# Hardware loops on VectorE and ScalarE, and an earlier V load for nine units, in a two-layer decode kernel

## The chip, the cores and the metric

One NeuronCore of one Trainium2 chip runs the whole program. The metric is the device time in microseconds (us) of one execution; the smaller the better. A program on one core has no second core to be compared with, so every run used here is one that was classed as fast (all executions of a kernel lie within 0.12% of each other). "The span" is the time of the one profiled execution; it is 1 to 2 us shorter than the timed runs.

## The reference, cut to what matters

Two layers of decoding for two sequences, one new token each. Attention over a cache of 16,384 positions in 32 heads dominates: every K and every V is read once per layer and used for one query only.

```python
B, Sq, D = 2, 1, 576
H, Sk, Dh = 32, 16384, 128
def _A_ref(x, k_cache, v_cache, wq, wo):
    q = (x @ wq).reshape(B, Sq, H, Dh)...          # transposed to b h q d
    scores = einsum("bhqd,bhkd->bhqk", q, k_cache) * (Dh ** -0.5)
    o = einsum("bhqk,bhkd->bhqd", softmax(scores), v_cache)
    return o... @ wo
x = x + A(layernorm(x));  x = x + B(layernorm(x))  # B: a small MLP with w1..w4
x = x + A(layernorm(x));  x = x + B(layernorm(x))  # the same caches and weights again
```

One (sequence, head) pair is called a unit: 64 units per layer, with 4 MB of K and 4 MB of V each (bfloat16).

## The kernel before

A unit's K is transposed on TensorE in chunks of 1024 positions, copied out by ScalarE (ACT) and multiplied with the query on TensorE; the remaining chunks are multiplied and summed on VectorE (DVE), two instructions per chunk. Then come the maximum, two exponentials on ACT, and the product with V on TensorE one unit later. SBUF holds three places for a K and a V each; K of a unit can be loaded only when the K that lay in its place has been used up.

The program is recorded as a list of operations for each engine and then emitted. TensorE's list is folded into a hardware loop of two units per turn; all other engines get straight-line code. That is the part that the change touches:

```python
ENGS = ("sync", "scalar", "tensor", "vector", "gpsimd")
...
with self.nc.Block() as block:
    for e in self.ENGS:
        def run(eng, items=plan[e], loops=self.loops if e == "tensor" else ()):
            at = 0
            for first, n, period, every, rest in loops:
                ...                                  # straight-line code up to unit `first`
                with eng.Fori(0, n) as turn:         # n turns of two units
                    for o, waits in self._fold(...):
                        self._run(eng, o, [(s, v + turn * d if d else v) for s, v, d in waits])
                    ...                              # every fourth turn: one piece of the wo product
            for o, waits in items[at:]:
                self._run(eng, o, waits)             # straight-line: the rest, or everything
```

The other part is the order of the loads. Layer 1 loads K of unit i, then V of unit i-1. Layer 2 starts with K and V of a unit together for the units 0 to EARLY-1 and then goes over to the order of layer 1; at that point one V is skipped, since it is there already:

```python
EARLY = 5
ROT = 7
...
for i in range(U):
    kv("K", l, i, ...)
    if l == 1 and i < self.EARLY:
        kv("V", l, i)
    elif i >= 1 and (l, i - 1) != (1, self.EARLY - 1):
        kv("V", l, i - 1)
...
def place(self, l, i):          # where K and V of unit i lie
    ...
    return (2, 0, 1)[i % 3] if i < self.ROT else (2, 1)[i % 2]
...
first = (2, self.ROT - 1)[l]    # TensorE's loop starts at unit 2 in layer 1, at unit 6 in layer 2
early = l == 1 and 1 <= i < self.EARLY   # V of unit i-1 is used in the middle of unit i
```

## Time and profile before

| | before |
|---|---|
| time, median of 6 runs | 2578.07 us (2577.16 to 2578.94) |
| span of the profiled run | 2576.8 us |
| read from HBM | 1097.7 MB |
| busy: DVE, PE, ACT | 68%, 64%, 48% of the span |
| rate in most of the 40 slices | 430 to 432 GB/s |

First, lines of the page: the span; what the 16 DMA engines moved in each of 40 equal slices; and the queues of part 3. Queue q1 is the data; q8 and q14, "instruction" by the page's name, carry the instructions that the engines fetch (packets, MB, share of the span of 16 DMA engines).

```profile
span 2576.8 us, 80453 instructions
...
GB/s 413 430 427 432 432 430 432 431 431 432 432 431 431 432 430 432 432 431 431 420 381 408 431 432 431 431 432 431 431 431 432 431 431 431 430 432 431 431 431 340
...
q1 hardware_dynamic: 46712, 1097.76, 99.4%
q8 instruction: 44, 0.72, 0.1%
q14 instruction: 38, 0.31, 0.0%
```

A flat rate: 431 GB/s but at the start, in slices 20 to 22, counted from 1 (the boundary of the layers and a hole 100 us later), and at the end. 1097.7 MB at 431 GB/s is 2547 us. In this trace no slice has more than 432 GB/s, and the packets of q1 take 99.4% of the time of the 16 DMA engines. The instruction queues: 1.03 MB, 0.1% of the DMA engines' time.

The chain of waits through one unit in the steady part (start, duration, what). It begins where a K landed and ends where the load that replaces it was issued, 14.54 us later. A unit takes 19.45 us to load, so compute has slack.

```profile
1440.24 1.89 PE tps L714 x16
...
1454.73 0.02 SPq L163
1454.75 0.03 issue
1454.78 25.70 DMA buf<-in_A_k_cache_dram
```

The same chain at the two ends: the last K of layer 1 lands at 1261.7 us and the last K of layer 2 at 2527.25 us (TensorE starts at once). From there a fixed tail of compute leads to the end at 2576.8.

```profile
1217.92 43.80 DMA buf<-in_A_k_cache_dram
1261.71 0.05 issue
1261.76 1.89 PE tps L714 x16
...
2484.40 42.85 DMA buf<-in_A_k_cache_dram
2527.25 0.05 issue
2527.30 1.89 PE tps L714 x16
```

The windows view of two holes in the loads (stretch, length; busy time and count of PE, PEld, DVE, ACT, POOL; clock, DMA share, GB/s). The first is the MLP between the layers, the second comes 100 us later:

```profile
1290.00:1295.00 5.00, 1.80 (x29) 1.68 (x30) 1.75 (x12) 1.00 (x4) 0.00 (x0) 0.50 0.28 113
1295.00:1300.00 5.00, 4.02 (x144) 3.90 (x141) 0.52 (x3) 0.49 (x2) 0.00 (x0) 0.50 0.48 130
1400.00:1405.00 5.00, 4.61 (x150) 4.35 (x148) 4.93 (x6) 3.36 (x5) 0.00 (x0) 0.84 0.89 377
1405.00:1410.00 5.00, 3.99 (x60) 3.79 (x61) 4.00 (x10) 2.16 (x3) 0.00 (x0) 0.50 0.69 233
```

What no view prints, but the trace holds: each load signals its semaphore sixteen times, and the sixteen times are recorded. The consumer waits for the last: TensorE started on layer 2's last K at 2527.30 us, 0.05 us after its last signal, the median one being 7.9 us older. I call the last signal minus the median one the lag of the latest DMA engine. It is worked out from these records:

```
before: landing of a load (us), and the largest three of the sixteen signals minus their median
  224.9   1.66  0.49  0.13        737.6   4.47  1.74  1.35       1252.1   8.34  3.38  1.76
  489.5   2.48  1.68  0.58        995.0   6.46  2.73  1.77       1310.6   1.61  0.65  0.36
  618.2   3.45  1.70  1.29       1131.9   7.41  3.46  1.80       2527.2   7.90  4.20  1.07
```

One DMA engine falls behind by one us every 128 us or so; at the layer boundary, where the queue runs empty, all catch up (lag 8.4 us at 1289.7, 0.6 at 1303.9), and in layer 2 it begins again. The records do not name the DMA engine of a signal or of a packet: that each of the sixteen signals stands for one of the sixteen engines, and that it is the same engine each time, is inferred from the sizes, which grow in steps.

### The profile page before, as it was taken

The numbers are of one execution on the slowest core, as the hardware profiler recorded it, in microseconds if no ns is written. First come the engines' busy times: TensorE is split into PE (matmuls) and PEld (weight loads), VectorE is DVE, ScalarE is ACT, GpSimd is POOL, SyncE is SP. The second block draws the span as 40 slices with busy tenths as digits, with TensorE's granted clock in tenths as the row PEclk, the third lists the DMA queues.
The fourth block names the chain that finished last, engine by engine and source line by source line (L and its number), as shares of the span: only waits on it lengthen the run. The fifth ranks groups of instructions, "written<-read, shape, count | busy, mean of one in ns | idle before, by whom it ended". The sixth has DMA issues, their size and how long they took to land.

```text
span 2576.8 us, 80453 instructions
## 1 busy us (share of the span) xinstructions
PE 1652.8 (64%) x36879; PEld 1540.8 (60%) x36879; DVE 1749.2 (68%) x2587; ACT 1231.9 (48%) x1941; POOL 0.8 (0%) x10
## 2 busy tenths in 40 slices
PE   5656665666666666666668666566656665666666
PEld 5656655665565656555668666555656565565555
DVE  5666776677666767766659777667766766677664
ACT  4444544454455445544436454445444544454443
POOL 0000000000000000000000000000000000000000
PEclk8666666676667666666656666666666766666666
DMA  9999999999999999999999999999999999999998
GB/s 413 430 427 432 432 430 432 431 431 432 432 431 431 432 430 432 432 431 431 420 381 408 431 432 431 431 432 431 431 431 432 431 431 431 430 432 431 431 431 340
DMA packets 46794, 1098.79 MB, mean 426 GB/s; under 512 B 4916, under 2 KB 6008, under 8 KB 11512
## 3 DMA queue, kind: packets, MB, share of 16 engines
q1 hardware_dynamic: 46712, 1097.76, 99.4%
q8 instruction: 44, 0.72, 0.1%
q14 instruction: 38, 0.31, 0.0%
HBM read 1097.74 MB, written 0.00 MB: 426 GB/s over the span
## 4 chain that ended last, share of the span: by engine, by line
DMA 60%; DVE 29%; PE 9%; issue 1%; ACT 0%; SPq 0%; DVEq 0%
DMA buf<-in_A_k_cache_dram 57%; DVE sd L746 18%; DVE prod L743 10%; PE tps L714 5%; DMA buf<-in_A_v_cache_dram 3%; PE misc L762 1%; PE ops L787 1%; DVE small L764 1%; DMA buf<-in_A_wq_dram 1%; PE sps L584 0%; PE misc L620 0%; ACT ktsb L718 0%; PE sps L731 0%; SPq L405 0%; PE misc L550 0%
## 5 line engine op out<-in xcount | busy, mean ns | idle before, releaser
L718 ACT ACTIVATE ktsb<-tps 128x1024 bf16<-128x1024 bf16 x1156 | 1125.1, 1031 | 872.2 <-PE tps L714 867.1
L714 PE MATMUL tps<-ident,buf 128*128 128x128 bf16 x9248 | 910.1, 262 | 635.0 <-DMA buf<-in_A_k_cache_dram 635.0
L714 PEld LDWEIGHTS tps<-ident,buf 128*128 128x128 bf16 x9248 | 733.7, 120 | 663.3 <-DMA buf<-in_A_k_cache_dram 655.4
L746 DVE TENSOR_REDUCE sd<-prod 128x8 f32<-128x1024 bf16 x892 | 1088.3, 1220 | 30.9
L743 DVE TENSOR_TENSOR prod<-buf,qb 128x1024 bf16<-128x1024 bf16 x892 | 607.9, 682 | 11.3 <-DMA buf<-in_A_k_cache_dram 10.3
L787 PE MATMUL ops<-p,buf 128*128 128x1 bf16 x16384 | 462.4, 164 | 74.9 <-DMA buf<-in_A_v_cache_dram 64.0
L787 PEld LDWEIGHTS ops<-p,buf 128*128 128x128 bf16 x16384 | 444.5, 100 | 84.9 <-DMA buf<-in_A_v_cache_dram 73.5
L764 DVE TENSOR_REDUCE small<-misc 128x1 f32<-128x128 f32 x128 | 37.4, 292 | 666.8 <-PE misc L762 666.8
L731 PE MATMUL sps<-qcur,ktsb 128*128 128x1 bf16 x9248 | 396.9, 166 | 108.8 <-ACT ktsb L718 88.3
L731 PEld LDWEIGHTS sps<-qcur,ktsb 128*128 128x128 bf16 x9248 | 349.0, 101 | 171.2 <-ACT ktsb L718 169.1
L698 ACT ACTIVATE qb<-misc 128x128 bf16<-128x128 f32 x128 | 35.5, 278 | 378.4 <-PE misc L695 378.4
L762 PE MATMUL misc<-identS,small 128*128 128x128 f32 x256 | 95.3, 476 | 13.5 <-DVE small L756 13.5
L762 PEld LDWEIGHTS misc<-identS,small 128*128 128x128 f32 x256 | 69.9, 334 | 15.3 <-DVE small L756 15.1
L773 ACT ACTIVATE p<-sps,small 128x72 bf16<-128x72 f32 (+1 forms) x128 | 41.5, 325 | 8.2 <-DVE small L764 8.2
L773 ACT ACTIVATE p<-sd,small 128x56 bf16<-128x56 f32 (+1 forms) x128 | 44.5, 348 | 0.0
L690 ACT ACTIVATE qcur<-qt 128x1 bf16<-128x1 bf16 x128 | 29.0, 227 | 19.6 <-DVE qt L627 19.6
L695 PE MATMUL misc<-ident,qcur 128*128 128x128 bf16 x128 | 34.2, 267 | 1.1 <-ACT qcur L690 1.1
L856 PE MATMUL misc<-lpiece,small 128*128 128x16 f32 x28 | 8.5, 384 | 36.7 <-DVE lpiece L854 36.7
L856 PEld LDWEIGHTS misc<-lpiece,small 128*128 128x128 f32 x28 | 7.0, 310 | 39.3 <-DVE lpiece L854 39.3
L752 DVE TENSOR_REDUCE small<-sps 128x1 f32<-128x72 f32 (+1 forms) x128 | 28.5, 222 | 0.0
L773 ACT ACTIVATION_READ_ACCUMULATOR p<-sps,small 128x1 f32 x128 | 27.1, 212 | 0.0
L773 ACT ACTIVATION_READ_ACCUMULATOR p<-sd,small 128x1 f32 x128 | 26.5, 207 | 0.0
(86 smaller groups left out, 223.0 us busy)
## 6 DMA issues: line engine op xcount, KB each, us to landing
buf<-in_A_k_cache_dram SPq DMA_DIRECT2D x124, 4096.0 KB, 24.3
buf<-in_A_v_cache_dram SPq DMA_DIRECT2D x124, 4096.0 KB, 34.0
buf<-in_B_w_dram SPq DMA_DIRECT2D x8, 1152.0 KB, 27.1
buf<-in_A_wq_dram SPq DMA_DIRECT2D x8, 1024.0 KB, 10.5
buf<-in_A_wo_dram SPq DMA_DIRECT2D x14, 576.0 KB, 34.6
buf<-in_A_k_cache_dram SPq DMA_DIRECT2D x3, 2048.0 KB, 15.6
buf<-in_B_w_dram SPq DMA_DIRECT2D x2, 2160.0 KB, 34.3
buf<-in_A_v_cache_dram SPq DMA_DIRECT2D x2, 2048.0 KB, 28.0
```

The lines of the kernel that those rows point to most:

```text
L690: self.act(lambda a: a.activation(out=self.qcur[:, q:q + 1], in_=self.qt[:, u:u + 1], func=ACT.Copy), r=["qt"], w=[f"qcur{q}"])
L695: self.pe(lambda pe: pe.matmul(self.misc[:, 0:128], lhsT=bcast(self.qcur[:, q:q + 1], 128), rhs=self.ident[:, :], start=True, stop=True), ...
L698: self.act(lambda a: a.activation(out=self.qb[q][:, :], in_=self.misc[:, 0:128], func=ACT.Copy), r=["P:misc"], w=[f"qb{q}"])
L714: ins = pe.transpose(self.tps[b][:, j * 128:(j + 1) * 128], kt[:, (j0 + j) * 128:(j0 + j + 1) * 128], self.ident[:, :])
L718: self.act(lambda a: a.activation(out=self.ktsb[k][:, :, :].rearrange("p a b -> p (a b)"), in_=self.tps[b][:, :], func=ACT.Copy), r=[f"P:t ...
L731: ins = pe.matmul(self.sps[sp][:, col:col + 1], lhsT=self.ktsb[k][:, j, :], rhs=self.qcur[:, sp:sp + 1], start=True, stop=True)
L743: self.dve(lambda v: v.tensor_tensor(out=self.prod[d][:, :, :], in0=k3, in1=bcast_mid(self.qb[q][:, :], self.CH), op=ALU.mult), r=[*res, f ...
L746: self.dve(lambda v: v.tensor_reduce(out=self.sd[q][:, o:o + self.CH], in_=self.prod[d][:, :, :], axis=AX.X, op=ALU.add), r=[f"prod{d}"], ...
L762: self.pe(lambda pe: pe.matmul(self.misc[:, 128:256], lhsT=bcast(self.m[:, q:q + 1], 128), rhs=self.identS[:, :], start=True, stop=True), ...
L764: self.dve(lambda v: v.tensor_reduce(out=self.bias[:, q:q + 1], in_=self.misc[:, 128:256], axis=AX.X, op=ALU.max, negate=True), r=["P:misc ...
L773: self.act(lambda a, c0=c0, c1=c1, src=src, part=part: a.activation(out=self.p[q][:, c0:c1], in_=src, func=ACT.Exp, bias=self.bias[:, q:q ...
L787: ins = pe.matmul(self.ops[q][:, 0:1], lhsT=vt[:, j * 128:(j + 1) * 128], rhs=self.p[q][:, h * self.TB + j:h * self.TB + j + 1], start=(h ...
```

## The change

The intent: VectorE and ScalarE also get hardware loops (all of a unit's column numbers that vary from turn to turn are held in registers), so that far fewer instructions have to be fetched; and layer 2 loads K and V together for nine units instead of five, to fill the second hole. The diff, cut to its core:

```diff
+    LOOPED = ("scalar", "tensor", "vector")
...
-                def run(eng, items=plan[e], loops=self.loops if e == "tensor" else ()):
+                def run(eng, items=plan[e], loops=self.loops if e in self.LOOPED else ()):
...
-                            for o, waits in self._fold([...]):
-                                self._run(eng, o, [(s, v + turn * d if d else v) for s, v, d in waits])
+                            for o, waits, u in self._fold([...]):
+                                self._run(eng, o, [(s, self._rise(v, turn, d)) for s, v, d in waits],
+                                          u and self._rise(u[0], turn, u[1]))
...
-    EARLY = 5
+    EARLY = 9
...
-        self.act(lambda a: a.activation(out=self.qcur[:, q:q + 1], in_=self.qt[:, u:u + 1], func=ACT.Copy), ...)
+        self.act(lambda a, u: a.activation(out=self.qcur[:, q:q + 1], in_=self.qt[:, bass.ds(u, 1)], ...), ..., u=u)
...                                       # likewise lsum, o, lpiece, opiece: columns from a register
-        first = (2, self.ROT - 1)[l]
+        first = (2, self.EARLY - 1)[l]   # so all loops of layer 2 start at unit 8 instead of 6
...
-            early = l == 1 and 1 <= i < self.EARLY
+            early = l == 1 and 1 <= i < first
```

More of the change, by code (lines that the diff above doesn't have):

```diff
@@ L15, with __init__ @@
 class Op:
-    __slots__ = ("eng", "fn", "deps", "need", "sem", "val", "clock", "at", "tag", "some", "own", "raw")
-    def __init__(self, eng, fn, at, tag, some):
-        self.eng, self.fn, self.at, self.tag, self.some = eng, fn, at, tag, some
+    __slots__ = ("eng", "fn", "deps", "need", "sem", "val", "clock", "at", "tag", "some", "own", "raw", "u")
+    def __init__(self, eng, fn, at, tag, some, u):
+        self.eng, self.fn, self.at, self.tag, self.some, self.u = eng, fn, at, tag, some, u
         self.deps, self.need, self.sem, self.val, self.clock = [], False, None, 0, None
@@ L43, in __init__ @@
         self.some = False
-        self.own = None
         self.loops = []
@@ L55, in _sem, with op @@
         return self.sems[name]
-    def op(self, eng, fn, r=(), w=(), deps=()):
-        o = Op(eng, fn, len(self.ops), self.tag, self.some)
-        if self.own and eng != "tensor":
-            o.own = f"{self.own}_{eng}"
+    def op(self, eng, fn, r=(), w=(), deps=(), u=None):
+        o = Op(eng, fn, len(self.ops), self.tag, self.some, u)
+        if self.some:
+            o.own = f"some_{eng}"
         self.ops.append(o)
@@ L144, in run @@
                             self._run(eng, o, waits)
+                        some = [[x for x in t if x[0].some] for t in turns]
+                        assert [t for t in range(n) if some[t]] in ([], list(range(rest, n, every)))
+                        assert all(o.some for t, c in zip(turns, some) for o, _ in t[len(t) - len(c):])
+                        some = [c for c in some if c]
                         with eng.Fori(0, n) as turn:
-                            for o, waits in self._fold([[x for x in t if not x[0].some] for t in turns]):
-                                self._run(eng, o, [(s, v + turn * d if d else v) for s, v, d in waits])
-                            some = [[x for x in t if x[0].some] for t in turns]
-                            assert [t for t in range(n) if some[t]] == list(range(rest, n, every))
-                            assert all(o.some for t, c in zip(turns, some) for o, _ in t[len(t) - len(c):])
-                            some = [c for c in some if c]
+                            for o, waits, u in self._fold([[x for x in t if not x[0].some] for t in turns]):
+                                self._run(eng, o, [(s, self._rise(v, turn, d)) for s, v, d in waits],
+                                          u and self._rise(u[0], turn, u[1]))
                             if some:
                                 with eng.If((turn + (every - rest)) % every == 0):
-                                    for o, waits in self._fold(some):
-                                        self._run(eng, o, [(s, v + (turn // every) * d if d else v) for s, v, d in waits])
+                                    for o, waits, u in self._fold(some):
+                                        k = turn // every
+                                        self._run(eng, o, [(s, self._rise(v, k, d)) for s, v, d in waits],
+                                                  u and self._rise(u[0], k, u[1]))
                         at = start + sum(map(len, turns))
@@ L159, in emit, with _rise, _run @@
                 getattr(block, e)(run)
-    def _run(self, eng, o, waits):
+    @staticmethod
+    def _rise(v, turn, d):
+        return v + turn * d if d > 0 else v - turn * -d if d else v
+    def _run(self, eng, o, waits, u=None):
         for s, v in waits:
             eng.wait_ge(self.sems[s], v)
-        ins = o.fn(eng)
+        ins = o.fn(eng) if o.u is None else o.fn(eng, o.u if u is None else u)
         if o.sem is not None:
@@ L195, in _fold @@
                 folded.append((s, first, d))
-            body.append((o, folded))
+            us = None
+            if o.u is not None:
+                us = o.u, same[1][0].u - o.u if len(same) > 1 else 0
+                assert all(p.u == us[0] + t * us[1] for t, (p, _) in enumerate(same))
+            body.append((o, folded, us))
         return body
@@ L317, in __init__ @@
         self.wolast = sb("wolast", [128, self.D], BF16)
-        self.lsum = sb("lsum", [128, self.U, 2], FP32)
+        self.lsum = sb("lsum", [128, 2 * self.U], FP32)
         self.o = sb("o", [128, self.U], FP32)
@@ L323, in __init__ @@
         self.lpiece = sb("lpiece", [128, 2 * self.wo_cols], FP32)
+        self.dpiece = sb("dpiece", [128, self.wo_cols], FP32)
         self.opiece = sb("opiece", [128, self.wo_cols], BF16)
@@ L349, in pe, with dve, act @@
     def pe(self, fn, r=(), w=()): return self.s.op("tensor", fn, r, w)
-    def dve(self, fn, r=(), w=()): return self.s.op("vector", fn, r, w)
-    def act(self, fn, r=(), w=()): return self.s.op("scalar", fn, r, w)
+    def dve(self, fn, r=(), w=(), u=None): return self.s.op("vector", fn, r, w, u=u)
+    def act(self, fn, r=(), w=(), u=None): return self.s.op("scalar", fn, r, w, u=u)
     def pool(self, fn, r=(), w=()): return self.s.op("gpsimd", fn, r, w)
@@ L689, in query @@
         u, q = self.order[l][i], i % 2
-        self.act(lambda a: a.activation(out=self.qcur[:, q:q + 1], in_=self.qt[:, u:u + 1], func=ACT.Copy),
-                 r=["qt"], w=[f"qcur{q}"])
+        self.act(lambda a, u: a.activation(out=self.qcur[:, q:q + 1], in_=self.qt[:, bass.ds(u, 1)], func=ACT.Copy),
+                 r=["qt"], w=[f"qcur{q}"], u=u)
     def query_rows(self, l, i):
@@ L772, in exps @@
                                                    (n, self.NB, self.sd[q][:, 0:self.NB - n], f"sd{q}"))):
-            self.act(lambda a, c0=c0, c1=c1, src=src, part=part: a.activation(
+            self.act(lambda a, u, c0=c0, c1=c1, src=src: a.activation(
                 out=self.p[q][:, c0:c1], in_=src, func=ACT.Exp, bias=self.bias[:, q:q + 1], scale=self.scale,
-                accum_out=self.lsum[:, u, part:part + 1]),
-                r=[res, f"bias{q}"], w=[f"p{q}", "lsum"])
+                accum_out=self.lsum[:, bass.ds(u, 1)]),
+                r=[res, f"bias{q}"], w=[f"p{q}", "lsum"], u=2 * u + part)
     def weigh(self, l, i, h):
@@ L793, in weigh @@
         if h == 1 and i < self.U - 1:
-            self.dve(lambda v: v.tensor_copy(out=self.o[:, u:u + 1], in_=self.ops[q][:, 0:1]),
-                     r=[f"P:ops{q}"], w=["o"])
+            self.dve(lambda v, u: v.tensor_copy(out=self.o[:, bass.ds(u, 1)], in_=self.ops[q][:, 0:1]),
+                     r=[f"P:ops{q}"], w=["o"], u=u)
     def normalizers(self, u0, u1):
@@ L800, in normalizers @@
         self.pe(lambda pe: pe.matmul(dps, lhsT=bcast(self.cone[:, :], 128),
-                                     rhs=self.lsum[:, u0:u1, :].rearrange("p u a -> p (u a)"),
+                                     rhs=self.lsum[:, 2 * u0:2 * u1],
                                      start=True, stop=True), r=["lsum", "consts"], w=["P:misc"])
@@ L851, in project_piece @@
         out = self.misc[:, 256:256 + KT * B]
-        den = self.den[:, u0:u1]
-        self.s.some, self.s.own = True, "piece"
-        self.dve(lambda v: v.tensor_copy(out=self.lpiece[:, :], in_=self.lsum[:, u0:u1, :].rearrange("p u a -> p (u a)")),
-                 r=["lsum"], w=["lpiece"])
+        den = self.dpiece[:, :]
+        self.s.some = True
+        self.dve(lambda v, u: v.tensor_copy(out=self.lpiece[:, :], in_=self.lsum[:, bass.ds(u, 2 * n)]),
+                 r=["lsum"], w=["lpiece"], u=2 * u0)
         self.pe(lambda pe: pe.matmul(dps, lhsT=bcast(self.cone[:, :], 128), rhs=self.lpiece[:, :], start=True,
@@ L858, in project_piece @@
         self.dve(lambda v: v.tensor_reduce(out=den, in_=dps.rearrange("p (u a) -> p u a", a=2), axis=AX.X,
-                                           op=ALU.add), r=["P:misc"], w=["den"])
-        self.dve(lambda v: v.reciprocal(out=den, in_=den), r=["den"], w=["den"])
-        self.dve(lambda v: v.tensor_tensor(out=self.opiece[:, :], in0=self.o[:, u0:u1], in1=den, op=ALU.mult),
-                 r=["den", "o"], w=["opiece"])
+                                           op=ALU.add), r=["P:misc"], w=["dpiece"])
+        self.dve(lambda v: v.reciprocal(out=den, in_=den), r=["dpiece"], w=["dpiece"])
+        self.dve(lambda v, u: v.tensor_tensor(out=self.opiece[:, :], in0=self.o[:, bass.ds(u, n)], in1=den, op=ALU.mult),
+                 r=["dpiece", "o"], w=["opiece"], u=u0)
         def rows(pe):
@@ L881, in project_piece @@
         self.pe(lambda pe: pe.nop(), w=["P:misc"])
-        self.s.some, self.s.own = False, None
+        self.s.some = False
     def attention(self, l):
```

## The prediction

> **What bounds the kernel now.** HBM loads. The page's slice table shows DMA at 9+ tenths and 430-432 GB/s in nearly every slice; 1097.7 MB at 431 GB/s is 2547 us of the 2577. DVE (68%), PE (64%) and ACT (48%) have slack: a unit takes 19.45 us of loading and 14.5 us of compute (chain of waits: K landed at 1440.24, the load that replaces it issued at 1454.78). So cheaper sequencing of DVE or ACT buys nothing by itself. Three things are lost beyond the bytes:
>
> 1. *One late DMA engine.* Each load signals sixteen times in the trace's landing records. The last signal trails the median one by 1.7 us at 240 us, then by one more us at about 440, 570, 698, 827, 954, 1083 and 1213 us, up to 8.3 us at the end of layer 1; it falls to 0.6 at the layer boundary (idle DMA) and climbs again from 1.4 us (1455) to 7.9 us (2527). The steps coincide with 8 KB packets of the instruction queue (page part 3, q14: 0.31 MB), about 128 us apart: straight-line code of DVE or ACT being fetched, each fetch costing some engine about 1 us. The last K of a layer lands when the latest engine is done, and a compute tail of 49.5 us follows it, so the lag is paid in full, twice.
> 2. *A hole at 1404-1410 us* (windows view: 377 and 233 GB/s in two 5-us windows). K of unit 7 replaces K of unit 5, which compute, catching up since 1320, released only at 1407.06; the landings there are 12.0 us apart instead of 9.7, so 2.3 us are lost.
> 3. *The boundary at 1290-1300 us* (113 and 130 GB/s), about 7 us: the first MLP. The change does not touch its cause.
>
> **What the change does.** Loops on DVE and ACT remove nearly all their fetches between units 2 and 61 of layer 1 and 8 and 61 of layer 2. TensorE already loops: its queue (q8) fetches nothing from 94 to 1250 us. [...] Cost: register arithmetic for waits and columns[...], against about 5 us of slack.
> EARLY 9 puts one more V between K5's landing and K7's issue, so compute has 29 us instead of 19.4; the tight spot moves to unit 10, where compute has caught up (16 us needed, about 20 available). Price: two more units unrolled on PE, five more 16 KB fetches, which seem to hardly add to the lag.
>
> **Sum.** Layer 1: lag 8.3 to about 1.9 us, -6.4. Hole: -2.3. Layer 2: lag 7.9 to about 2.3, -5.6. Total -14.3 us, all on the critical path since DMA is saturated and the tails only shift. 2578.5 - 14.3 = 2564.
>
> Predicted 2564 us, range 2559 to 2573. Chances: faster by over 2% 0.01, within 2% 0.96, slower 0.03.
>
> **Right or wrong in the profile.** Right: q14 falls from about 38 packets to under 15; landing lag stays under 3 us in both layers; 430+ GB/s at 1400; last K of layer 1 lands 6 us earlier; unit compute stays under 17 us; PE, DVE and ACT busy times unchanged. Wrong if q14 rises[...]; if the lag stays (it comes from something else: then only 2 us gained); if a hole appears near unit 10; or if the DVE/ACT register work lengthens a unit beyond the slack.

-6.4, -2.3 and -5.6 make the -14.3 us. That the bodies are fetched once rests on TensorE's loop in the trace alone: nothing on q8 from 94 to 1250 us.

## The result

| | before | after |
|---|---|---|
| median of 6 runs | 2578.07 us | 2565.85 us (2564.95 to 2566.82) |
| ratio, 95% interval | | 0.9953, 0.9940 to 0.9966 |
| span | 2576.8 us | 2565.0 us |

Ratios here and below are the mean time of one kernel's fast runs over that of the other's of the same rounds, so not quite the ratio of the medians that are quoted. The change is clear of noise: 12.2 us.

The page after: the span, the slices and the queues.

```profile
span 2565.0 us, 84163 instructions
...
GB/s 414 429 429 431 432 433 430 431 432 432 430 432 431 432 432 432 432 431 431 424 413 429 423 418 432 431 433 431 432 431 432 431 431 433 431 431 431 433 431 375
...
q1 hardware_dynamic: 46712, 1097.76, 99.8%
q8 instruction: 48, 0.79, 0.1%
q14 instruction: 10, 0.08, 0.0%
```

q14 went from 38 packets to 10; q8 from 44 to 48: I read it as TensorE's queue, and the four packets as the two more units that it now runs straight-line. (The trace does not name the engine of a packet. Looping VectorE or ScalarE changes q14 alone, in e1 to e3; in e5 against e4, with two more units straight-line, only q8 rises, from 44 to 48.) The bytes saved, 0.16 MB net, are worth 0.4 us at 431 GB/s. That isn't where 12 us come from.

The last K of layer 1 in the chain of waits, and TensorE's first transposes of layer 2's last K (from the view of the tile, whose last two times are first and last start):

```profile
1212.21 42.92 DMA buf<-in_A_k_cache_dram
1255.13 0.05 issue
1255.17 1.89 PE tps L726 x16
```

```profile
L726 PE MATMUL tps<-ident,buf x36: 268/314/314, 2515.3 to 2520.0; 128*128 128x128 bf16 x36
```

Layer 1's last K lands 6.6 us earlier, layer 2's 12.0 us earlier (at 2515.25), and the tail to the end is nearly as long as it was (49.5 and 49.8 us). The landing records show the lag gone:

```
after: landing of a load (us), and the largest three of the sixteen signals minus their median
  224.9   1.79  0.41  0.32        734.8   1.86  0.39  0.38       1245.5   2.00  1.81  0.32
  488.6   1.82  0.38  0.37        990.2   1.87  0.40  0.38       2515.3   1.93  1.49  1.15
```

The windows of the two holes, and four where there was none before:

```profile
1290.00:1295.00 5.00, 2.99 (x113) 2.90 (x110) 1.26 (x4) 0.49 (x2) 0.00 (x0) 0.50 0.82 273
1295.00:1300.00 5.00, 3.31 (x124) 3.23 (x122) 0.00 (x0) 0.00 (x0) 0.00 (x0) 0.50 1.04 423
1400.00:1405.00 5.00, 2.53 (x41) 2.27 (x40) 2.70 (x6) 1.43 (x3) 0.00 (x0) 0.50 0.98 416
1405.00:1410.00 5.00, 4.73 (x82) 4.58 (x80) 3.68 (x5) 4.70 (x9) 0.00 (x0) 0.72 1.00 433
1455.00:1460.00 5.00, 1.07 (x39) 0.88 (x35) 4.12 (x9) 0.28 (x1) 0.00 (x0) 0.56 0.95 377
1475.00:1480.00 5.00, 2.02 (x75) 1.84 (x72) 4.90 (x9) 0.28 (x1) 0.00 (x0) 0.61 0.95 378
1480.00:1485.00 5.00, 1.86 (x41) 1.60 (x42) 1.20 (x7) 0.00 (x0) 0.00 (x0) 0.50 0.94 380
1500.00:1505.00 5.00, 3.94 (x52) 3.88 (x53) 4.00 (x10) 2.73 (x4) 0.00 (x0) 0.50 0.97 360
```

The hole at the boundary, now some 6 us earlier, looks smaller. As I read it, that is the average over the engines: those that had waited there for the late one now have less to wait for, and the latest engine gains nothing by it (table below, second row). The hole at 1405 is filled, and three shallow dips have come at the loads of K 10, 11 and 12. The timeline of the DMA queue has their issues: K 9 and K 10 (two in one line), V 9, K 11, V 10, K 12.

```profile
1437.81 20.05 SPq L403 DMA_DIRECT2D buf<-in_A_k_cache_dram  x2
1457.91 0.42 SPq L403 DMA_DIRECT2D buf<-in_A_v_cache_dram  x1
1478.45 0.33 SPq L403 DMA_DIRECT2D buf<-in_A_k_cache_dram  x1
1478.83 0.42 SPq L403 DMA_DIRECT2D buf<-in_A_v_cache_dram  x1
1499.31 0.33 SPq L403 DMA_DIRECT2D buf<-in_A_k_cache_dram  x1
```

K 9 landed at 1463.9 and the load that replaces it was issued 14.6 us later, about as fast as in the kernel before (14.54): the register arithmetic of the loops costs a unit nothing that the trace shows. The DMA engines, though, were up to 5.3 us apart at that time (first to last of sixteen signals), while TensorE's straight-line units were being fetched until 1485. My reading is that these fetches set them apart and that the engines that were ahead had run out of work; e5 and e6 below do not settle it.

Where the time went, in the landing of the same loads on the latest engine. The kernel before and the changed one were each traced twice (e7 and e8 below turned out to be the same programs again), which shows the scatter:

| stretch (us) | before | again | after | again |
|---|---|---|---|---|
| last K of layer 1 lands at | 1261.7 | 1261.6 | 1255.1 | 1255.6 |
| from there to V 2 of layer 2 | 77.5 | 76.9 | 77.9 | 78.0 |
| V 2 to K 12 (the hole, the dips) | 180.2 | 179.4 | 180.8 | 180.2 |
| from K 12 to the last K of layer 2 | 1007.9 | 1008.1 | 1001.4 | 1001.6 |

So there are two gains of 6.0 to 6.6 us, one in each layer's steady part, and none at all where the order of the loads was changed. (The hole itself varies from one execution to the next: the two landings at it are 12.0 us apart in the first trace of the kernel before, 11.2 in the second, and 9.7 where there is no hole.)

### The profile page after: what moved, and what is told of

It reads as the page before. It is cut to its first block, busy times and chain, and to the rows that moved or that the text cites. A ratio compares the mean times of both kernels' runs of the same rounds, so it can differ in the third digit from the quotient of the medians.

```text
span 2565.0 us, 84163 instructions
## 1 busy us (share of the span) xinstructions
PE 1652.4 (64%) x36879; PEld 1539.2 (60%) x36879; DVE 1750.1 (68%) x2587; ACT 1229.8 (48%) x1941; POOL 0.8 (0%) x10
## 4 chain that ended last, share of the span: by engine, by line
DMA 57%; issue 16%; DVE 16%; PE 8%; SPq 1%; ACT 1%; DVEq 0%
DMA buf<-in_A_k_cache_dram 56%; DVE prod L755 12%; PE tps L726 5%; DVE sd L758 3%; PE misc L774 2%; SPq L434 1%; PE ops L799 1%; DMA buf<-in_B_w_dram 1%; DMA buf<-in_A_wq_dram 1%; SPq L417 0%; ACT ktsb L730 0%; PE misc L632 0%; DVE small L776 0%; PE sps L596 0%; PE sps L743 0%
## 5 line engine op out<-in xcount | busy, mean ns | idle before, releaser
L755 DVE TENSOR_TENSOR prod<-buf,qb 128x1024 bf16<-128x1024 bf16 x892 | 607.5, 681 | 11.1 <-DMA buf<-in_A_k_cache_dram 10.2
L774 PE MATMUL misc<-identS,small 128*128 128x128 f32 x256 | 95.3, 476 | 12.2 <-DVE small L768 12.2
L702 ACT ACTIVATE qcur<-qt 128x1 bf16 (+1 forms) x128 | 29.2, 228 | 19.6 <-DVE qt L639 19.6
L785 ACT ACTIVATION_READ_ACCUMULATOR p<-sps,small (+1 forms) x128 | 27.3, 213 | 0.0
L785 ACT ACTIVATION_READ_ACCUMULATOR p<-sd,small (+1 forms) x128 | 26.6, 208 | 0.0
```

The costliest lines, as they stand in the source:

```text
L702: self.act(lambda a, u: a.activation(out=self.qcur[:, q:q + 1], in_=self.qt[:, bass.ds(u, 1)], func=ACT.Copy), r=["qt"], w=[f"qcur{q}"], u=u)
L755: self.dve(lambda v: v.tensor_tensor(out=self.prod[d][:, :, :], in0=k3, in1=bcast_mid(self.qb[q][:, :], self.CH), op=ALU.mult), r=[*res, f ...
L774: self.pe(lambda pe: pe.matmul(self.misc[:, 128:256], lhsT=bcast(self.m[:, q:q + 1], 128), rhs=self.identS[:, :], start=True, stop=True), ...
L785: self.act(lambda a, u, c0=c0, c1=c1, src=src: a.activation(out=self.p[q][:, c0:c1], in_=src, func=ACT.Exp, bias=self.bias[:, q:q + 1], sc ...
```

## The experiments

Theory A: an instruction fetch of an engine lands on one DMA engine that serves it; in a kernel whose sixteen DMA engines never idle, that one falls behind by about one us per fetch, and every load waits for the latest of the sixteen. Lags count as the maximum over the DMA engines, not as a sum. Which DMA engine serves a fetch is not recorded; the theory is tested by what it says of times, packets and lags. Rival B: fetched bytes simply cost bandwidth. Rival C: it's the sequencing of VectorE and ScalarE that got faster. Theories D and E concern the load order.

All runs gave the reference's result. Each had five timed rounds, except the change itself (six runs); the runs of before in the three sets had medians of 2578.26, 2577.72 and 2577.56 us.

### e1: the ScalarE loop undone

```diff
-    LOOPED = ("scalar", "tensor", "vector")
+    LOOPED = ("tensor", "vector")
```

> The change with the ScalarE loop undone (ScalarE again straight-line, VectorE looped, nine units loaded together). Theory A (each engine's instruction fetches fall on one DMA engine of its own, and the load lands with the latest of the sixteen, so lags count as the maximum, not the sum): VectorE's lag (8 us at a layer's end) is gone, ScalarE's (the second latest, 4.2 us in the trace before) becomes the latest. So about 2 to 2.5 us per layer are lost against the full change: 2570 us, lag at the last K of a layer about 4.2 us, steps about 0.7 us every 150 us. Rival B (fetch packets simply cost DMA bandwidth, shares add up): 0.36 MB in all is 0.8 us of 2578, so this run would equal the change within 0.5 us: 2566. Rival C (the gain comes from faster sequencing in the loops, not from fetches): lag unchanged at 8 us.

Measured: 2569.22 us (2568.89 to 2570.09), ratio 0.9967. Lag at the last K: 4.0 us in layer 1, 3.6 in layer 2.

```profile
q14 instruction: 22, 0.18, 0.0%
```

As theory A has it: the second-latest engine of the trace before (4.3 and 4.2 us behind at the last K of the two layers) is now the latest. It rose by 0.7 us at each fetch. (Of the q14 packets in the trace before, those of about 325 ns, some 128 us apart, coincide with the steps of one us, and those of about 309 ns, some 165 us apart, with the steps of 0.7 us. Which belong to VectorE and which to ScalarE is inferred from this run and the next.) Rival B's equal time and rival C's unchanged lag are out.

### e2: the VectorE loop undone

```diff
-    LOOPED = ("scalar", "tensor", "vector")
+    LOOPED = ("scalar", "tensor")
```

> The change with the VectorE loop undone (VectorE straight-line, ScalarE looped, nine units together). Theory A: the latest DMA engine is the one that fetches for VectorE, so looping ScalarE alone gains nothing: lag at the last K still 7.5 to 8.5 us in both layers, time 2577 to 2579, and the gains of e1 and e2 do not add up to that of the change (8 + 0 against 12). Rival B (shares add): a part of the gain in proportion to the bytes, some 40% of it, 2573.

Measured: 2576.10 us (2575.38 to 2576.39), ratio 0.9992. Lag 8.6 us in layer 1, 6.5 in layer 2.

```profile
q14 instruction: 26, 0.21, 0.0%
```

This is 1 us less than I had expected, and layer 2's lag is below the 7.5 to 8.5 us that I had expected; but it must be compared with e3, which differs from it only in the ScalarE loop: 2576.10 against 2576.00. Looping ScalarE alone, with 12 packets of q14 saved, gains nothing, as long as VectorE's fetches hold the latest engine back. The packets add up (16 saved in e1, 12 in e2, 28 with both), the times don't: against e3, VectorE's loop alone gains 6.8, ScalarE's alone 0, both 10.2 us (the last against the change's own set of runs).

### e3: nine units loaded together, no loops

```diff
-    LOOPED = ("scalar", "tensor", "vector")
+    LOOPED = ("tensor",)
```

> Only the other half of the change: nine units of layer 2 load K and V together, VectorE and ScalarE stay straight-line. My prediction gave this half 2.3 us (2576). After reading the trace of the change I expect less: the hole near 1405 us went, but smaller dips came at units 10 to 12, and two more units unrolled on TensorE brought the latest engine a lag of 4.0 us by 1485. Theory A with that: within 1 us of before, 2577 to 2579.

Measured: 2576.00 us (2575.69 to 2576.69), ratio 0.9993. By the medians this half is worth 2.3 us by itself, the very number of my prediction, and not the 0 that I expected after seeing the trace of the change. The ranges of the runs do not overlap (the runs of before: 2576.76 to 2578.84), but the 95% interval of the ratio, 0.9979 to 1.0007, includes 1, so the size is uncertain. But the trace doesn't show it where I had put it: the stretch with the hole took 179.7 us here, against 180.2 and 179.4 in two traces of before. The steady stretch after it took 1006.6 instead of 1008, and the lag at the last K of layer 2 is 6.3 instead of 7.9 us. VectorE fetches eight times in that stretch in both. Yet the lag shows seven steps of one us before and only six in e3 (and in e2, which has the same order). A reading that fits, but that no run tests: the queue running dry lets a late engine catch up, here the dips come late, at 1460 to 1490 us (down to 328 GB/s), the old hole came at 1405, and one fetch more of VectorE (at 1445) would be forgiven.

### e4: loops, five units together

```diff
-    EARLY = 9
+    EARLY = 5
...
-        first = (2, self.EARLY - 1)[l]
+        first = (2, 6)[l]
...
-            early = l == 1 and 1 <= i < first
+            early = l == 1 and 1 <= i < max(self.EARLY - 1, 5)
```

> Loops on VectorE and ScalarE with the old five units loaded together and the old loop start (unit 6). If the load order gave its predicted 2.3 us, this is 2568. If the hole was only moved, it is 2565 to 2566.5, like the change; the hole at about 1398 us is then there again with 12 us between two landings, and TensorE's fetches end earlier, with a lag below 3 us at 1490.

Measured: 2565.47 us (2565.02 to 2567.36), ratio 0.9954: the loops alone give all of the change's gain. The hole is there again, at about half the size that it had in the first trace of the kernel before:

```profile
1395.00:1400.00 5.00, 3.72 (x143) 3.64 (x143) 4.93 (x6) 1.76 (x2) 0.00 (x0) 0.73 0.86 364
1400.00:1405.00 5.00, 5.00 (x73) 4.68 (x71) 4.01 (x9) 3.32 (x5) 0.00 (x0) 0.59 0.94 357
```

Two landings there are 10.9 us apart, not the 12 that I expected from the kernel before; in the second trace of before (e7) they were 11.2, so one trace each says little about the difference. The two halves of the change aren't additive: 12.8 (loops) and 2.3 (order) make 12.2 together.

### e5: as e4, but the loops of layer 2 start at unit 8

```diff
-        first = (2, 6)[l]
+        first = (2, 8)[l]
```

> Loops with five units loaded together, but the loops of layer 2 start at unit 8 as in the change, so TensorE (and the others) run two more units straight-line; nothing else differs from e4. It tells the load order and the unrolling apart, which the change mixes. Theory D (the hole at 1400 hides the lag of TensorE's fetches; without a hole the lag is paid): with the hole still there the extra fetches after it cost 0.5 to 1.5 us, 2566 to 2567. Rival E (TensorE's fetches cost nothing, the dips at units 10 to 12 alone eat the gain): same as e4, 2565.5.

Measured: 2566.45 us (2565.47 to 2568.39), ratio 0.9957. The median is 1.0 us above e4's, but the ranges overlap, so by time this is inconclusive. In the trace the last K of layer 2 lands 1.7 us later than in e4 (2515.25 against 2513.59), and one landing right after the hole, where e4 has 10.0 us, is 11.2 us after the one before it, with the lag going from 1.9 to 3.5. One trace each, with a scatter of up to 1.2 us between two traces of one program, supports theory D but doesn't prove it.

### e6: loops, seven units together

```diff
-    EARLY = 9
+    EARLY = 7
```

> Loops with seven units loaded together, loop start at unit 6: a V is moved ahead of the hole without unrolling more. Theory D: the hole moves by two units and shrinks, the lag stays as in e4; 2564.5 to 2565.5, so at most 1 us better than e4. Rival E (the dips follow the switch of the order wherever it is and cost 2.5 us): 2565.5 or more, with dips at units 8 to 10.

Measured: 2566.91 us (2565.57 to 2567.41), ratio 0.9958. No better than e4 or the change. The dip sits at 1415 to 1425 (396 and 387 GB/s), and a lag of 2.6 to 3.2 us after it stays to the end of the layer. Moving the switch of the order moves the dip; it gains nothing. Theory D had said 2564.5 to 2565.5 and the lag of e4 (1.5 us); both were missed, and the time is as rival E has it. TensorE fetches no more here than in e4 (q8 has 44 packets in both), so the extra fetches of e5 and of the change cannot be the whole reason why the order gains nothing with the loops in.

### e7 and e8: an experiment that failed

```diff
             self.row_max(l, i)
+            if (2, 8)[l] <= i < U - 2:
+                for _ in range(20):
+                    self.dve(lambda e: e.nop())
```

> The kernel before, with 20 empty instructions at the end of every unit's VectorE program (units 2 to 61 and 8 to 61), where VectorE idles: it doubles the instructions that VectorE has to fetch and nothing else. Theory A: fetch packets of VectorE twice as dense (every 64 us), the lag of the latest DMA engine about 17 us at the last K of layer 1 and 15 us at that of layer 2, so 2578 + 9 + 8 = 2595 us, DVE still far from full. Rival C (fetches do not matter, VectorE has slack): 2578 to 2580.

> The same 20 empty instructions per unit in the changed kernel, inside the VectorE loops: executed as often as in e7, but fetched once. Theory A: 2566 as the change, within 1 us, q14 at about 10 to 12 packets. If the time that the empty instructions take were what slows e7, this run would be slower by the same 17 us.

Measured: 2578.18 us (ratio 1.0003) and 2566.05 us (0.9955). That would refute theory A, but the pages count exactly the instructions and q14 packets of the kernels before and after (80453 and 38; 84163 and 10): the empty instructions were dropped when the program was built. The two runs only measure how well a time and a trace repeat. e9 and e10 do it with real instructions.

### e9: twice as many VectorE instructions in the kernel before

```diff
             self.row_max(l, i)
+            if (2, 8)[l] <= i < U - 2:
+                for k in range(20):
+                    at = self.otn[:, i % 2 * 32 + k:i % 2 * 32 + k + 1]     # not in use until unit 62
+                    self.dve(lambda v, at=at: v.memset(at, 0.0))
```

> What e7 was meant to be (its empty instructions were dropped by the compiler, so e7 and e8 were the kernels before and after once more): the kernel before with 20 one-column memsets of a dead tile at the end of every unit on VectorE, in its idle time. Twice as many VectorE instructions to fetch. Theory A: a fetch every 64 us instead of 128, each 1 us on one DMA engine, so the lag at the last K about 17 us in layer 1 and 15 us in layer 2; 2578 + 9 + 8 = 2595 us. Rival C (VectorE has slack, fetches do not matter): 2578 to 2580.

Measured: 2594.71 us (2594.24 to 2595.49), ratio 1.0066: 17.2 us slower, 2595 expected. The queue, and the memsets in the view of groups (count, then busy us in all and mean ns of one):

```profile
q14 instruction: 56, 0.46, 0.0%
```

```profile
L928 DVE MEMSET otn<- 128x1 bf16 x2280 | 35.6, 59 | 1.0
```

35.6 us of work over the whole span, in VectorE's idle time, and 18 more packets of 8 KB. VectorE's fetches came every 60 to 70 us. One number was wrong: the lag stopped at 13.0 and 12.6 us instead of 17 and 15. A reading that fits: the engines that were ahead ran out of work (422 and 420 GB/s between 1000 and 1100 us), so the median waits, too, and lag measured against it no longer shows all of the delay. The last K of layer 1 landed at 1271.3, 9.6 us later than before.

### e10: the same memsets inside the changed kernel's loops

The edit is that of e9, made to the changed kernel.

> The same 20 memsets per unit in the changed kernel, inside the VectorE loops (body about 120 instructions instead of 80). Executed as often as in e9, fetched once. Theory A: 2566, within 1 us of the change, instruction packets as there. If it is the time of the memsets that slows e9, this run is slower by as much as e9.

Measured: 2565.48 us (2565.04 to 2566.19), ratio 0.9954, the time of the change.

```profile
q14 instruction: 11, 0.09, 0.0%
```

```profile
L940 DVE MEMSET otn<- 128x1 bf16 x2280 | 39.9, 59 | 1.5 <-issue 0.3
```

The same 2280 memsets were executed and cost nothing. What cost 17 us in e9 was that they had to be fetched.

### e11: straight-line work on GpSimd in the changed kernel

```diff
+        self.junk = sb("junk", [128, 8], BF16)
+        self.pool_before = []
...                                       # self.last_max is VectorE's row maximum of the unit
             self.row_max(l, i)
+            if (2, 8)[l] <= i < U - 2:
+                for k in range(20):
+                    at = self.junk[k % 4 * 32:k % 4 * 32 + 32, k // 4:k // 4 + 1]
+                    o = self.s.op("gpsimd", lambda g, at=at: g.memset(at, 0.0),
+                                  deps=[] if k else [self.last_max, *self.pool_before])
+                self.pool_before = [o]
```

> The changed kernel with 20 small memsets per unit on GpSimd, straight-line, paced by VectorE's row maximum; nothing waits for them. Theory A (any engine's straight-line code delays the DMA engine that serves its fetches): one DMA engine lags by 7 or 8 steps of 0.7 to 1 us in each layer, 5 to 8 us at the last K instead of 1.9 and 1.5, and the time goes back to 2572 to 2578 although GpSimd takes no part in the work. Rival C (only the sequencing of engines in the chain counts): 2566.

Measured: 2572.42 us (2572.10 to 2573.15), ratio 0.9981; lag at the last K 5.1 us in layer 1 and 5.4 in layer 2, in steps of about 0.68 us.

```profile
q14 instruction: 29, 0.24, 0.0%
```

```profile
L942 POOL MEMSET junk<- 32x1 bf16 x2280 | 215.2, 94 | 2285.2 <-DVE small L770 2204.2
```

Nothing in the kernel waits for GpSimd, and it's idle nine tenths of the time; yet its 19 packets give back half of the change's gain, at the lower edge of what was expected. This is the plainest run for theory A: it needs no engine of the chain. The same GpSimd work in a loop was not run; that the fetches and not the memsets delay the loads rests on the steps, which come at the packets (after those at 826.6, 945.0 and 1063.7 us the lag is 3.2, 3.9 and 4.6 us).

### e12: a loop body of 200 instructions

The edit is that of e10, with 60 memsets per unit (into two tiles not in use, one for even and one for odd units).

> The changed kernel with 60 memsets per unit on VectorE inside the loops: a body of about 200 instructions[...]. [...] no refetch, instruction packets as in the change, and only the memsets' own time[...]: 2566 to 2569. [...]

Measured: 2565.95 us (2565.44 to 2566.35), ratio 0.9954.

```profile
q14 instruction: 12, 0.10, 0.0%
```

No refetching: 12 packets, at an estimated 13 KB of code per turn (200 instructions of about 65 bytes: in e9, 2280 memsets more took 18 packets of 8,192 bytes more). The memsets took 1.5 us of VectorE's time per unit (168.8 us in 114 units). The case's own loops are shorter, about 80 (VectorE, an estimate) and 60 (ScalarE) instructions; longer ones on these two engines were not run.

None of the versions tried beats the change clearly: e4, e10 and the change lie within 0.4 us of each other.

## Why the prediction was right, and where it was not

The predicted time was 2564 us in a range of 2559 to 2573; measured 2565.85. Point by point:

- *What bounds the kernel: loads.* Right. Adding 2280 instructions to VectorE in a loop changed nothing (e10, 2565.48 us); 19 fetch packets for an engine without a part in the work cost 6.6 us against the change's median (e11).
- *One late DMA engine, one us per fetch, paid in full twice.* Right, and shown: doubling the fetches (e9) took the time from 2577.6 to 2594.7. Layer 1: predicted -6.4, measured -6.6 (last K at 1261.7 and 1255.1). Layer 2's steady part: predicted -5.6, measured -6.5 (1007.9 and 1001.4).
- *"straight-line code of DVE or ACT": which of the two was left open.* It's VectorE. ScalarE's fetches hold back another DMA engine, as I read the steps, by 0.7 us each, and count only once VectorE's are gone: looping ScalarE gains 3.4 us with VectorE looped (e1: 2569.22, the change: 2565.85) and nothing without (e2: 2576.10, e3: 2576.00).
- *The loop bodies are fetched once.* Right: q14 fell to 10 packets. They are smaller than the 100 to 150 instructions that I had estimated: in the trace of the change a turn executes on average 69 instructions on VectorE (an estimated 80 with the piece that runs every fourth turn) and 60 on ScalarE.
- *"register arithmetic for waits and columns".* None shows in the trace: 14.5 us before and 14.6 after from a K's landing to the issue of the load that replaces it.
- *"Hole: -2.3".* This is the step that failed. The hole was filled, but the stretch from V 2 to K 12 took 180.8 and 180.2 us instead of 180.2 and 179.4. With the loops in, five units together (e4) are as fast as nine. Of the marks named in advance, "430+ GB/s at 1400" was missed (416), and "a hole appears near unit 10" came true in a shallow form (the dips at K 10 to 12). Two sub-steps were wrong. "about 20 available" at unit 10 left out that the DMA engines are up to 5.3 us apart there, so that, as I read it, those ahead run dry first. And "five more 16 KB fetches, which seem to hardly add to the lag": the lag reached 4.0 us at 1485, where I had said it would stay below 3. That these fetches cost about 1 us is supported by e5, within the scatter, but e6 gained nothing without them; which of the dips and the fetches eats the gain stays open.
- *Without the loops* the order did give some 2 us (e3), but not in the stretch that I named. Why it is worth that there, and how much exactly, is not settled.

So the sum came out 2 us too good: -14.3 predicted, -12.2 measured. In the first two traces the stretches changed by -6.6 (to layer 1's last K), +0.4 (the boundary), +0.6 (the hole and the dips), -6.5 (after them) and +0.2 us (the tail). The hole's term is 2.9 us off; that the sum is not as far off is in part luck, since the two steady parts gave 1.1 us more than predicted.

## What to carry to other kernels

In a kernel that keeps all DMA engines busy, look at when the sixteen signals of a load arrive, not only at GB/s: the load is there when the latest engine is done, and here that was up to 8.4 us after the median one at an average rate of 431 GB/s that showed nothing of it. Straight-line code of VectorE, of ScalarE and even of GpSimd, which has no part in the work, made one DMA engine late at each fetch: in the steady parts an 8 KB packet took 0.31 to 0.33 us by its own record (kernel before), and the lag grew by 1.0 us (VectorE) or 0.7 us (ScalarE, and GpSimd in e11). (For TensorE's 16 KB fetches the traces are mixed: after 16 of them between 1338 and 1443 us the lag was 1.4 us in the kernel before; in the changed kernel it reached 4.0 us while they went on.) Loop the engine whose fetches make the latest engine first (VectorE here: e1 is 6.8 us faster than e3), and expect nothing from the second until that's done (e2: 0). And a hole in the loads need not be a loss of its full size: late engines may use it to catch up, as at the layer boundary here, where the lag fell from 8.4 to 0.6 us. Ask what the latest engine does in it before counting it.
